# Routed rows withheld at the end of two outer stages, and a folded forward transform for two sequences

## The chip, the cores and the metric

The kernel runs on one core of one Trainium2 chip. The metric is the device time of one execution in microseconds. The kernel before took 2111.44 us, the median of three runs (2107.42 to 2115.52).

## What is computed

A long convolution over four sequences of 11456 positions and 128 channels (u = x v, convolved with a filter that a small MLP makes of position embeddings, the result multiplied by x), and a mixture of eight experts on the 45824 rows that come out, each row going to the one expert with the highest gate logit:

```python
h_filt = (np.maximum(pos_emb @ w1, 0.0) @ w2) * np.exp(-0.01 * pos)[:, None]
u = x * v
y = np.fft.irfft(np.fft.rfft(u, n=2 * S, axis=1) * np.fft.rfft(h_filt, n=2 * S, axis=0)[None], n=2 * S, axis=1)[:, :S]
x = (x * y).reshape(B * S, D)

logits = x @ w_gate + modality_bias[modality_id]
e_idx = np.argmax(logits, axis=1)
gate_w = softmax(logits)[np.arange(N), e_idx]
for e in range(E):
    h = np.maximum(x[e_idx == e] @ w1[e], 0.0)
    out[e_idx == e] = gate_w[e_idx == e, None] * (h @ w2[e])
```

## The kernel before, in words

The transform is cut into 90 x 64 and done as matmuls. The program is a row of stages. Filter stages make the filter; `filter_middle` (23 groups) writes its spectrum. Then for each sequence b an *outer* stage of 16 steps and a *middle* stage of 23 groups follow: outer 0 (the forward transform of sequence 0, laid under `filter_middle` with its loads and products), middle 0, outer 1, middle 1, outer 2, middle 2, outer 3, middle 3, outer 4, and last the expert tiles, in which 512 sorted rows at a time run through an expert's two matrices.

An outer stage b has two halves of work in each step. Of sequence b it does the forward transform (`forward_stages`): loads of u and v, `product` on DVE (L490), matmuls against the table `fwd` (L505, in `transform`, 64 instructions a step in two halves of 32), and the copy of each half out of PSUM by ACT (L508). Of sequence b - 1 it does the inverse transform (`inverse_stages`: turns L730, matmuls into `py` L739, ACT's copy L742, the sum and difference of the halves and the product with x on DVE, L743, L745, L746) and the routing (`route_stages`: L778 to L883; POOL's part are the gate's bias and the shift, L808 and L810; TensorE's transposes are L778 and L801).

The forward matmul takes its input with all 128 partitions; two of its 128 x 64 tiles lie side by side in the array.

A middle stage's group multiplies by the spectrum: matmuls L646, products on DVE (L663, L670) and POOL (L665, L666, L676, L677), inverse matmuls L701, copies L707.

Routing gives each row of a sequence its place in the sorted array `xs`. The rows go there by indirect DMAs that POOL issues, 90 for each sequence (`send_rows`, L283), each of 128 rows; they are loaded back first, five at a time (L263, here called `back`). How many rows go at which point is written by hand: `paced(x, n)` sends n rows that wait for instruction x. `product` sends two or three, the inverse transform two in each step, the last one also three in every second; some steps of the middle stages send more; and the loop over the expert tiles sends one in every second chunk for the first tiles, then one in every third:

```python
def paced(x, n=1):
    send_rows(n, wait=ins_of(x))
```

The order on TensorE, ACT, DVE and SP is the one in which the code is written, step by step: the tables `OUTER`, `LAST` and `FIRST` say at which step after its start each piece of work is done, and the place in the table says the order within a step. POOL's order is made by a scheduler.

In the expert loop each tile loads its rows (SP, L1121 for the tiles known early, L1125 and L1126 for the others), transposes them (L1210 on TensorE in the first tiles, L1212 on DVE later), and runs the matmuls. The results go out over DVE, SP's `y`, POOL's product with the gate weight (L1290) and four indirect DMAs (L1292, issued by POOL too). A load of x waits for the rows that may lie in it. After the last rows SP writes pads behind each expert's rows (L1052 and nine of L1060, in `rest`), and the x loads of later tiles stand behind these pads in SP's queue.

Of the kernel before, what the change touches and what calls it, by code (L numbers as in the profile page):

```python
# [48 lines left out]
def surely_full(n):  # L49
# [6 lines left out]
RW = D + 2  # L56
NOWHERE = 1 << 20
OUTER = ("turn0:2 turn1:2 lturn:5 biased:5 send:6 half:4 forward:3 load_x:0 product:2 choice:5 "
         "inverse:2 logits:4 shift:4 load:0 store:6 places:7")
LAST = ("lturn:5 biased:5 send:6 turn0:1 choice:5 turn1:1 inverse:2 logits:4 half:3 shift:4 load_x:0 store:5 places:6")  # L60
FOUT = "load:0 hidden:2 transform:3"
FMID = "turn:0 spectrum:1 second:3"
FIRST = "forward load product"
EA = 3
F1, F2 = 1, 24
UNSURE = 5
# [1 line left out]
NDYN = 8  # L68
NA, NXO = 12, 3
NPE = 9  # L70


def apart(a, axis):
# [116 lines left out]
def hyena_moe_kernel(ctx: ExitStack, tc: tile.TileContext, a: dict, out: bass.AP,  # L190
# [188 lines left out]
    with ExitStack() as cv:  # L379
# [93 lines left out]
        def forward_stages(b):  # L473
            kept = {}

            def load(q):
                for name in ("u", "v"):
                    if b == 0 and name == "v":
                        of = xo_t[q // 2 % NXO].rearrange("p w s h r -> p (w s h r)")
                        t = of[:, 1024 * (q % 2):1024 * (q % 2) + 1024]  # L480
                    else:
                        t = new_a((name, q))
                    kept[q, name] = t
                    sp.dma_start(t[0:D:2], a[name][b, q, 0:D // 2])
                    sp.dma_start(t[1:D:4], a[name][b, q, D // 2:])

            def product(q):

                u = kept[q, "u"]
                s = dve.scalar_tensor_tensor(u, u, sm("held")[:, 0:1], kept.pop((q, "v")),  # L490
                                             op0=ALU.mult, op1=ALU.mult)
                paced(s, 2 + (q % 2 == 0))
                if b:
                    free(("v", q))

            def transform(q):

                u = kept.pop((q, "u")).rearrange("p (b d n) -> p b d n", b=2, n=N2)
                for h in range(2):
                    p = pair("s1")  # L500
                    v = p[:, :, 0:4 * N1].rearrange("p b (d k) -> p b d k", d=4)
                    for j in range(4):
                        for blk in range(2):
                            for c in range(2):
                                pe.matmul(v[64 * c:64 * c + 64, blk, j], u[:, blk, 4 * h + j],  # L505
                                          fwd[:, c], start=True, stop=True)
                    d0 = 8 * q + 4 * h
                    act.copy(A.rearrange("p k b d -> p b k d")[:, :, :, d0:d0 + 4],  # L508
                             v.rearrange("p b d k -> p b k d"))
                free(("u", q))  # L510

            return load, product, transform

        def filter_stages():

# [201 lines left out]
        def inverse_stages(b):  # L717
# [15 lines left out]
            def transform(q):  # L733


                py = pair("py")
                for c in range(2):
                    for blk in range(2):
                        pe.matmul(py[64 * blk:64 * blk + 64, c], inv[:, c], w_of(q, blk)[:, c],  # L739
                                  start=True, stop=True)  # L740
                y = new_a(("y", q))
                act.copy(y[:, 512:1024], py[:, 1])  # L742
                paced(dve.tensor_add(y[:, 0:512], py[:, 0], y[:, 512:1024]),  # L743
                      1 + (b == nb - 1 and q % 2))
                dve.tensor_sub(y[:, 512:1024], py[:, 0], y[:, 512:1024])  # L745
                paced(dve.tensor_mul(xo_of(b, q // 2)[:, :, q % 2, :, 0:D], four(y),  # L746
                                     four(kept.pop(q))))
                free(("x", q), ("y", q))

            return load, turn, transform  # L750
# [147 lines left out]
        def outer_steps(b):  # L898
# [11 lines left out]
                    "choice": every_other(choice), "send": every_other(send),  # L910
                    "store": every_other(store), "places": every_other(places)}
            if b < nb:
                load, product, transform = forward_stages(b)
                todo |= {"load": load, "product": product, "forward": transform}
            if b == nb:
                todo.pop("places")
                for name, n in (("half", 2), ("logits", 2), ("lturn", 4), ("biased", 4), ("choice", 4),
# [9 lines left out]
                    lambda late: None, lambda late: (send(o), places(o))])  # L927
            if b == 0:
                ahead = lambda q: 2 * q if q < NA else q + F2 - NA
                when = {"load": ahead, "product": lambda q: ahead(q) + 2, "forward": lambda q: q + F2 - 1}  # L930
                return steps(NQ, [(when[n], todo[n]) for n in FIRST.split()])
            table = [w.split(":") for w in (LAST if b == nb else OUTER).split()]

# [157 lines left out]
    def experts(lo, hi):  # L1091
# [212 lines left out]
        for at in range(len(work) + 6):  # L1304
# [7 lines left out]
                finale[at - FL](late)  # L1312
            if lo == 0 and at >= FL + len(finale) + 2 and len(waiting) <= RC and not fetched:
                fetched.append(fetch(nb - 1))
            if lo == 0 and c % (2 if i < 12 else 3) == 0:
                send_rows(1)
            if lo == 0 and 1 <= i and c % 3 == 0:
                whole_weights(1)
# [31 lines left out]

def device_inputs(inputs):
    arrays = {name: np.ascontiguousarray(inputs[name]) for name in _INS}
    tile4 = lambda a: a.reshape(D, 2, NQ, 4, -1).transpose(2, 0, 1, 3, 4).reshape(NQ, D, -1)
    held = np.r_[0:D:2, 1:D:4]
    chan8 = lambda a: (apart(a.reshape(2, 64, 2, N2, NQ, 8), 1).transpose(4, 2, 1, 0, 5, 3)
                       .reshape(NQ, D, -1)[:, held])
    for name, of, order in (("x", "x", tile4), ("u", "x", chan8), ("v", "v", chan8)):
        arrays[name] = np.ascontiguousarray(
            np.stack([order(spread(np.asarray(a))) for a in inputs[of]]))

    pos = apart(spread(np.asarray(inputs["pos_emb"])).reshape(2, 64, 2, NQ, 4, -1), 1)
    arrays["pos_emb"] = np.ascontiguousarray(
# [24 lines left out]
```

## Time and profile before

| | before |
|---|---|
| median of three runs | 2111.44 us (2107.42 to 2115.52) |
| the profiled execution | 2110.57 us, span 2108.7 us, granted clock 0.986 of full speed |
| PE busy | 2022.3 us, 96% |
| weight loads (PEld) | 1653.7 us, 78% |
| DVE busy | 1675.1 us, 79% |
| ACT busy | 1192.9 us, 57% |
| POOL busy | 1369.1 us, 65% |
| HBM | 179 GB/s over the span |

The span runs from the first to the last instruction of the profiled execution; its own time is 1.9 us longer. Busy shares are averages over stages that differ: POOL's 65%, for instance, is made of stretches in which it has next to nothing to do and others in which it issues DMAs without a break.

### The profile page before, as it was taken

The numbers are of one execution on the slowest core, as the hardware profiler recorded it, in microseconds if no ns is written. First come the engines' busy times: TensorE is split into PE (matmuls) and PEld (weight loads), VectorE is DVE, ScalarE is ACT, GpSimd is POOL, SyncE is SP. The second block draws the span as 40 slices with busy tenths as digits, with TensorE's granted clock in tenths as the row PEclk, the third lists the DMA queues.
The fourth block names the chain that finished last, engine by engine and source line by source line (L and its number), as shares of the span: only waits on it lengthen the run. The fifth ranks groups of instructions, "written<-read, shape, count | busy, mean of one in ns | idle before, by whom it ended". The sixth has DMA issues, their size and how long they took to land. (4 is left out here: it accounts for less than half of the span.)

```text
span 2108.7 us, 49645 instructions
## 1 busy us (share of the span) xinstructions
PE 2022.3 (96%) x17794; PEld 1653.7 (78%) x17794; DVE 1675.1 (79%) x2663; ACT 1192.9 (57%) x2174; POOL 1369.1 (65%) x1496
## 2 busy tenths in 40 slices
PE   8999999999978999699999999999999999999997
PEld 8887877777757877488668888888888888888897
DVE  2538867996767967497887899988999999899885
ACT  3642476226631266223766666666666666666775
POOL 2219600796778876787667887888888665555554
PEclk9999999999989999899999999999999999999998
DMA  9846766678975788666689466666655554554310
GB/s 290 304 167 237 244 205 185 229 250 271 286 234 190 255 267 278 195 228 215 182 261 305 106 132 131 133 133 134 136 132 125 122 113 96 100 99 99 81 41 30
DMA packets 502932, 380.74 MB, mean 181 GB/s; under 512 B 374745, under 2 KB 408365, under 8 KB 502681
## 3 DMA queue, kind: packets, MB, share of 16 engines
q1 hardware_dynamic: 470265, 294.16, 51.0%
q0 software_dynamic: 32256, 83.33, 11.8%
q8 instruction: 142, 2.33, 0.4%
q14 instruction: 109, 0.89, 0.1%
q10 hardware_dynamic: 160, 0.03, 0.0%
HBM read 273.80 MB, written 103.96 MB: 179 GB/s over the span
## 5 line engine op out<-in xcount | busy, mean ns | idle before, releaser
L1240 DVE SCALAR_TENSOR_TENSOR hl<-ph,hh 128x512 fp32r<-128x512 f32 x724 | 484.7, 680 | 93.9 <-ACT hh L1239 85.0
L1239 ACT ACTIVATE hh<-ph 128x512 fp32r<-128x512 f32 x724 | 424.5, 598 | 200.9 <-PE ph L1236 193.1
L283 POOL DMA_INDIRECT xs<-back,to x360 | 389.4, 1082 | 175.8 <-issue 87.2
L1292 POOL DMA_INDIRECT out<-ot,idx x362 | 392.1, 1083 | 128.6 <-issue 82.0
L1234 PE MATMUL ph<-xh,wh 128*128 128x512 f32 (+1 forms) x792 | 298.5, 377 | 1.1 <-ACT xh L1220 1.1
L1236 PE MATMUL ph<-xl,wh 128*128 128x512 f32 (+1 forms) x792 | 296.1, 374 | 2.4 <-DVE xl L1221 2.4
L1235 PE MATMUL ph<-xh,wl 128*128 128x512 f32 (+1 forms) x792 | 294.4, 372 | 1.0 <-DVE wl L1189 1.0
L1257 PE MATMUL po<-hh,wh 128*128 128x512 f32 (+1 forms) x792 | 294.4, 372 | 0.0
L1259 PE MATMUL po<-hl,wh 128*128 128x512 f32 (+1 forms) x792 | 293.9, 371 | 0.0
L1258 PE MATMUL po<-hh,wl 128*128 128x512 f32 (+1 forms) x792 | 293.7, 371 | 0.0
L701 PE MATMUL pw<-rings,a 64*128 64x128 f32 x3952 | 242.1, 278 | 38.0 <-POOL a L676 33.9
L701 PEld LDWEIGHTS pw<-rings,a 64*128 64x128 f32 x3952 | 230.6, 191 | 57.3 <-POOL a L676 36.4
L707 ACT COPY A<-pw 128x512 f32<-128x512 f32 x180 | 95.7, 584 | 317.7 <-PE pw L701 317.7
L670 DVE TENSOR_TENSOR a<-pz,rings 128x1024 f32<-128x1024 f32 (+1 forms) x184 | 211.5, 1191 | 1.0 <-POOL a L677 1.0
L646 PE MATMUL pz<-A,rings 128*64 128x256 f32 x1440 | 170.0, 384 | 13.4 <-issue 8.9
L1236 PEld LDWEIGHTS ph<-xl,wh 128*128 128x128 f32 x792 | 149.4, 189 | 31.0 <-DVE xl L1221 3.5
L505 PE MATMUL s<-fwd,a 128*64 128x90 f32 x4096 | 170.1, 242 | 1.2 <-issue 1.1
L1235 PEld LDWEIGHTS ph<-xh,wl 128*128 128x128 f32 x792 | 149.6, 189 | 26.3 <-DVE wl L1189 1.3
L1234 PEld LDWEIGHTS ph<-xh,wh 128*128 128x128 f32 x792 | 149.4, 189 | 26.3 <-ACT xh L1220 1.3
L1257 PEld LDWEIGHTS po<-hh,wh 128*128 128x128 f32 x792 | 149.1, 188 | 26.0 <-issue 0.7
L1259 PEld LDWEIGHTS po<-hl,wh 128*128 128x128 f32 x792 | 149.1, 188 | 25.8
L1258 PEld LDWEIGHTS po<-hh,wl 128*128 128x128 f32 x792 | 149.1, 188 | 25.3
(192 smaller groups left out, 3537.7 us busy)
## 6 DMA issues: line engine op xcount, KB each, us to landing
rings<-hs SPq DMA_DIRECT2D x88, 512.0 KB
a<-in_x SPq DMA_DIRECT2D x64, 512.0 KB
xr<-xo SPq DMA_DIRECT2D x64, 365.6 KB
back<-xr POOLq DMA_DIRECT2D x72, 325.0 KB
rings<-in_c_b SPq DMA_DIRECT2D x88, 256.0 KB
rings<-in_c_c SPq DMA_DIRECT2D x88, 256.0 KB
x<-xs SPq DMA_DIRECT2D x292, 64.0 KB
ob<-oT SPq DMA_DIRECT2D x292, 64.0 KB
```

The costliest lines, as they stand in the source:

```text
L283: s = pool.indirect_dma_start(out=xs, out_offset=bass.IndirectOffsetOnAxis(ap=ix, axis=0), in_=src, in_offset=None, bounds_check=E * R - 1 ...
L670: dve.tensor_mul(part[i], z[:, :, i].unsqueeze(1).broadcast_to([D, 2, n, 2, D]), h[:, 0].unsqueeze(3).broadcast_to([D, 2, n, 2, D]))
L701: pe.matmul(pw[par][:, to:to + D], t[at], k["c"][at, q, c], start=i == 0, stop=i == len(terms) - 1)
L1234: pe.matmul(p, k[0, "h"][:, f:f + D], k["xh"], start=True, stop=False)
L1235: pe.matmul(p, k[0, "l"][:, f:f + D], k["xh"], start=False, stop=False)
L1236: pe.matmul(p, k[0, "h"][:, f:f + D], k["xl"], start=False, stop=True)
L1239: act.activation(hh, ph, AF.Relu)
L1240: dve.scalar_tensor_tensor(hl, ph, 0.0, hh.bitcast(F32), op0=ALU.max, op1=ALU.subtract)
L1257: pe.matmul(po, k[1, "h"][:, f], hh[:, t], start=g == 0, stop=False)
L1258: pe.matmul(po, k[1, "l"][:, f], hh[:, t], start=False, stop=False)
L1259: pe.matmul(po, k[1, "h"][:, f], hl[:, t], start=False, stop=g == NCH - 1)
L1292: s = pool.indirect_dma_start(out=out, out_offset=bass.IndirectOffsetOnAxis(ap=k["idx"][:, j:j + 1], axis=0), in_=ot[:, j, :], in_offset=N ...
```

## The change

Three things.

- `QS = 13`: steps 13 to 15 of outer 2 and outer 3 send no rows (neither from `product` nor from the inverse transform); those of outer 4 go on, at three in each step.
- The expert loop sends a row in every second chunk for the first 28 tiles, not 12.
- `FOLDED = 2`: for sequences 0 and 1 the host lays the two halves of a step's data beside each other, with one half's order turned. After `product`, POOL subtracts them (128 x 512), and DVE makes the sum of them (`total`, 128 x 512, as 2 times the one minus the difference). The forward matmuls take 64 partitions each, in four 64 x 64 tiles of the array instead of two of 128 x 64. There are as many of them as before.

```diff
 OUTER = ("turn0:2 turn1:2 lturn:5 biased:5 send:6 half:4 forward:3 load_x:0 product:2 choice:5 "
-         "inverse:2 logits:4 shift:4 load:0 store:6 places:7")
+         "inverse:2 total:2 logits:4 shift:4 load:0 store:6 places:7")
-FIRST = "forward load product"
+FIRST = "forward load product total"
+FOLDED = 2
+QS = 13
...
                 s = dve.scalar_tensor_tensor(u, u, sm("held")[:, 0:1], kept.pop((q, "v")),
                                              op0=ALU.mult, op1=ALU.mult)
-                paced(s, 2 + (q % 2 == 0))
+                paced(s, 2 + (q % 2 == 0) if q < QS else 0)
                 if b:
                     free(("v", q))
+                if b < FOLDED:
+                    pool.tensor_sub(u[:, 512:1024], u[:, 0:512], u[:, 512:1024])
+
+            def total(q):
+
+                u = kept[q, "u"]
+                if b < FOLDED:
+                    dve.scalar_tensor_tensor(u[:, 0:512], u[:, 0:512], 2.0, u[:, 512:1024],
+                                             op0=ALU.mult, op1=ALU.subtract)
...
                             for c in range(2):
-                                pe.matmul(v[64 * c:64 * c + 64, blk, j], u[:, blk, 4 * h + j],
-                                          fwd[:, c], start=True, stop=True)
+                                if b < FOLDED:
+                                    at = slice(64 * blk, 64 * blk + 64)
+                                    x, w = u[at, c, 4 * h + j], fwd[at, c]
+                                else:
+                                    x, w = u[:, blk, 4 * h + j], fwd[:, c]
+                                pe.matmul(v[64 * c:64 * c + 64, blk, j], x, w, start=True, stop=True)
...
-                paced(dve.tensor_add(y[:, 0:512], py[:, 0], y[:, 512:1024]),
-                      1 + (b == nb - 1 and q % 2))
+                n = 1 if b == nb - 1 or q < QS else 0
+                paced(dve.tensor_add(y[:, 0:512], py[:, 0], y[:, 512:1024]), n + (b == nb - 1))
                 dve.tensor_sub(y[:, 512:1024], py[:, 0], y[:, 512:1024])
                 paced(dve.tensor_mul(xo_of(b, q // 2)[:, :, q % 2, :, 0:D], four(y),
-                                     four(kept.pop(q))))
+                                     four(kept.pop(q))), n)
...
-                when = {"load": ahead, "product": lambda q: ahead(q) + 2, "forward": lambda q: q + F2 - 1}
+                when = {"load": ahead, "product": lambda q: ahead(q) + 2,
+                        "total": lambda q: ahead(q) + 3, "forward": lambda q: q + F2 - 1}
...
-            if lo == 0 and c % (2 if i < 12 else 3) == 0:
+            if lo == 0 and c % (2 if i < 28 else 3) == 0:
                 send_rows(1)
...
+    def chan8(a, b):
+        a = apart(a.reshape(2, 64, 2, N2, NQ, 8), 1)
+        if b < FOLDED:
+            a = np.stack([a[0], a[1][:, ::-1]]).transpose(4, 0, 1, 2, 5, 3)
+        else:
+            a = a.transpose(4, 2, 1, 0, 5, 3)
+        return a.reshape(NQ, D, -1)[:, held]
```

How the order moves, at three places. A row names the line, the operation, what it writes and reads, and how many alike stand together.

POOL, from the end of outer 2 to the first products of middle 2 (`xs<-back` is a routed row, `back<-xr` the load of five, L808 and L810 belong to the routing, `a` are the products' tiles). Before, rows stand up to the first product of group 0:

```order
L283 DMA xs<-back_95,to_92 373248x130 x2
L808 TENSOR_TENSOR lg<-wf,bias 109x128
L810 TENSOR_TENSOR lg<-lg,flagged 109x128
L283 DMA xs<-back_95,to_92 373248x130
L808 TENSOR_TENSOR flagged<-wf,bias 109x128
L283 DMA xs<-back_96,to_92 373248x130 x2
L263 DMA back_94<-xr_58 128x650
L283 DMA xs<-back_96,to_92 373248x130 x3
L283 DMA xs<-back_94,to_92 373248x130 x2
```

In the changed kernel:

```order
L285 DMA xs<-back_95,to_92 373248x130 x2
L265 DMA back_96<-xr_58 128x650
L285 DMA xs<-back_95,to_92 373248x130 x2
L823 TENSOR_TENSOR lg<-wf,bias 109x128
L825 TENSOR_TENSOR lg<-lg,flagged 109x128
L823 TENSOR_TENSOR flagged<-wf,bias 109x128
L823 TENSOR_TENSOR lg<-wf,bias 109x128
L825 TENSOR_TENSOR lg<-lg,flagged 109x128
L680 TENSOR_TENSOR a_125<-a_125 128x256
L681 TENSOR_TENSOR a_125<-a_125 128x256
L691 TENSOR_TENSOR a_128<-a_128,a_131 128x512
```

The rows have gone from between the routing's operations; five of these stand ahead of the first product (L665 before, L680 now).

DVE, one step of outer 1 (L490 is the product, `py` the inverse transform's result in PSUM, `xo` the step's output). Before:

```order
L743 TENSOR_TENSOR a10_133<-py_3611,a10_133 128x512
L745 TENSOR_TENSOR a10_133<-py_3611,a10_133 128x512
L746 TENSOR_TENSOR xo1_89<-a10_133,a6_129 128x2x4x128
L817 TENSOR_TENSOR lg_3626<-lt_3660,lg_3626 109x128
L490 SCALAR_TENSOR_TENSOR a0_123<-a0_123,small_81,a9_132 128x1024
```

In the changed kernel:

```order
L492 SCALAR_TENSOR_TENSOR a10_133<-a10_133,small_81,a0_123 128x1024
L759 TENSOR_TENSOR a5_128<-py_3445,a5_128 128x512
L760 TENSOR_TENSOR a5_128<-py_3445,a5_128 128x512
L761 TENSOR_TENSOR xo0_88<-a5_128,a9_132 128x2x4x128
L504 SCALAR_TENSOR_TENSOR a10_133<-a10_133 128x512
L832 TENSOR_TENSOR lg_3461<-lt_3495,lg_3461 109x128
L492 SCALAR_TENSOR_TENSOR a11_134<-a11_134,small_81,a2_125 128x1024
```

`total` (L504) works on the product of the same step (tile a10) and stands behind the three operations of the inverse.

POOL, expert tiles between the twelfth and the twenty-seventh. Before, three rows stand between two tiles (the last three operations of one tile are the cast of its indices L1280, the product L1290 and the four output DMAs L1292):

```order
L283 DMA xs_66<-back2_96,to1_93 373248x130 x3
L1280 CAST idx_20462<-ends_20233 128x4
L1290 TENSOR_TENSOR ot_20343<-y_20295,ends_19770 128x512
```

In the changed kernel four:

```order
L285 DMA xs_66<-back0_94,to0_92 373248x130 x2
L285 DMA xs_66<-back1_95,to0_92 373248x130 x2
L265 DMA back2_96<-xr2_60 128x650
L1296 CAST idx_15386<-ends_15147 128x4
L1306 TENSOR_TENSOR ot_15260<-y_15212,ends_14673 128x512
L1308 DMA out_0<-ot_15260,idx_14913 45824x128 x4
```

Eighteen rows more lie in this loop than before: 177 instead of 159 of the 360.

## Rows read from the trace of the kernel before

**Rows 1.** The page, busy tenths of PE in 40 equal slices of the span

```profile
PE   8999999999978999699999999999999999999997
```

**Rows 2.** Timeline of PE: start us, us, engine, line, operation, output<-inputs, count [idle before <-releaser]

```profile
369.40 0.47 PE L801 MATMUL lt<-ident,lT_late 128*109 128x128 f32 x2 [0.64 <-ACT lT_late L795]
...
483.61 0.34 PE L730 MATMUL wt<-ident,A 128*90 128x128 f32 x1 [0.61 <-DVE A L707]
...
604.63 0.36 PE L801 MATMUL lt<-ident,lT_late 128*109 128x128 f32 x1 [0.64 <-ACT lT_late L795]
...
637.41 0.58 PE L701 MATMUL pw<-rings,a 64*128 64x128 f32 x2 [16.58 <-POOL a L676]
...
736.54 0.34 PE L730 MATMUL wt<-ident,A 128*90 128x128 f32 x1 [0.64 <-DVE A L707]
...
857.60 0.36 PE L801 MATMUL lt<-ident,lT_late 128*109 128x128 f32 x1 [0.64 <-ACT lT_late L795]
...
988.71 0.34 PE L730 MATMUL wt<-ident,A 128*90 128x128 f32 x1 [0.64 <-DVE A L707]
```

**Rows 3.** Timeline of POOL and DVE at the start of middle 2

```profile
596.42 0.98 POOL L283 DMA_INDIRECT xs<-back,to  x1 [0.30 <-DVE score L833]
...
613.62 0.67 DVE L663 TENSOR_TENSOR a<-pz,rings 128x512 f32<-128x512 f32 x1
...
632.89 0.74 POOL L665 TENSOR_TENSOR a<-a 128x256 f32<-128x256 f32 x1
```

**Rows 4.** Timeline of POOL, SP and DVE in the expert tiles

```profile
1207.37 0.60 POOL L263 DMA_DIRECT2D back<-xr  x1
...
1212.65 1.03 POOL L1290 TENSOR_TENSOR ot<-y,ends 128x512 f32<-128x512 f32 x1
...
1636.91 0.97 POOL L283 DMA_INDIRECT xs<-back,to  x1 [0.30 <-issue]
...
1638.04 1.04 POOL L1290 TENSOR_TENSOR ot<-y,ends 128x512 f32<-128x512 f32 x1
...
1640.17 0.37 SPq L1052 DMA_DIRECT2D xs<-pad  x1
...
1663.47 0.71 DVE L1212 STREAM_TRANSPOSE xT<-x 128x512 f32<-128x512 f32 x1 [1.11 <-DMA x<-xs]
```

**Rows 5.** Timeline of SP, POOL and PE at the start of the expert tiles

```profile
1067.09 0.33 SPq L1121 DMA_DIRECT2D x<-xs  x1
...
1072.27 0.46 POOL L810 TENSOR_TENSOR bs_late<-bs_late,flagged 109x128 f32<-109x128 f32 x1
...
1072.65 0.66 PE L1210 MATMUL px<-ident,x 128*128 128x128 f32 x4
```

**Rows 6.** Groups by line, 95 to 160 us: count | busy, mean ns | idle before, releaser

```profile
L505 PE MATMUL s<-fwd,a 128*64 128x90 f32 x1024 | 40.4, 241 | 1.2 <-issue 1.1 <-DVE rings L609 0.2
L508 ACT COPY A<-s 128x720 f32<-128x720 f32 x32 | 24.3, 760 | 17.0 <-PE s L505 17.0
...
L676 POOL TENSOR_TENSOR a<-a,a 128x512 f32<-128x512 f32 x3 | 3.8, 1266 | 0.7 <-DVE a L670 0.7
```

**Rows 7.** Timeline of PE, ACT and DVE in outer 1

```profile
302.65 1.89 PE L739 MATMUL py<-rings,inv 90*64 90x512 f32 x8
...
304.59 0.59 ACT L742 COPY a<-py 128x512 f32<-128x512 f32 x1 [0.96 <-PE py L739]
305.21 0.70 DVE L743 TENSOR_TENSOR a<-py,a 128x512 f32<-128x512 f32 x1 [2.35 <-ACT a L742]
...
306.67 1.23 DVE L746 TENSOR_TENSOR xo<-a,a 128x1024 f32<-128x1024 f32 x1
...
308.46 2.70 PE L505 MATMUL s<-fwd,a 128*64 128x90 f32 x64
...
324.32 0.92 PE L505 MATMUL s<-fwd,a 128*64 128x90 f32 x18
```

**Rows 8.** Groups by line, first from 385 to 440 us, then from 295 to 330

```profile
L877 DVE TENSOR_TENSOR score<-score,oh 109x128 f32<-109x128 f32 x2 | 3.3, 1668 | 0.0
...
L877 DVE TENSOR_TENSOR score<-score,oh 109x128 f32<-109x128 f32 x2 | 0.6, 284 | 0.0
```

More of the change, by code (lines that the diff above doesn't have):

```diff
@@ L510, in transform @@
                 free(("u", q))
-            return load, product, transform
+            return load, product, total, transform
         def filter_stages():
@@ L912, in outer_steps @@
             if b < nb:
-                load, product, transform = forward_stages(b)
-                todo |= {"load": load, "product": product, "forward": transform}
+                load, product, total, transform = forward_stages(b)
+                todo |= {"load": load, "product": product, "total": total, "forward": transform}
             if b == nb:
@@ L1352, in device_inputs @@
     arrays = {name: np.ascontiguousarray(inputs[name]) for name in _INS}
-    tile4 = lambda a: a.reshape(D, 2, NQ, 4, -1).transpose(2, 0, 1, 3, 4).reshape(NQ, D, -1)
+    tile4 = lambda a, b: a.reshape(D, 2, NQ, 4, -1).transpose(2, 0, 1, 3, 4).reshape(NQ, D, -1)
     held = np.r_[0:D:2, 1:D:4]
-    chan8 = lambda a: (apart(a.reshape(2, 64, 2, N2, NQ, 8), 1).transpose(4, 2, 1, 0, 5, 3)
-                       .reshape(NQ, D, -1)[:, held])
+    def chan8(a, b):
[5 more added lines that the diff above has]
+        return a.reshape(NQ, D, -1)[:, held]
     for name, of, order in (("x", "x", tile4), ("u", "x", chan8), ("v", "v", chan8)):
         arrays[name] = np.ascontiguousarray(
-            np.stack([order(spread(np.asarray(a))) for a in inputs[of]]))
+            np.stack([order(spread(np.asarray(a)), b) for b, a in enumerate(inputs[of])]))
     pos = apart(spread(np.asarray(inputs["pos_emb"])).reshape(2, 64, 2, NQ, 4, -1), 1)
```

## Prediction

> **What bounds the kernel now.** I read first the line of busy tenths over the span: PE is full, nine tenths or more, from the eighteenth of the forty slices on, which holds the end of middle 3, the last outer stage and all expert tiles but the end, and dips in slices 12, 13 and 17 [rows 1]. So TensorE bounds the kernel, and time can come back only where it stands still: in those dips, and in stretches where a faster matmul shortens PE's own work.
>
> Then the timeline of PE at both ends of each middle stage [rows 2]. From the last step of an outer stage (L801) to the first of the next (L730) it takes 483.61 - 369.40 = 114.2 us in middle 1, 736.54 - 604.63 = 131.9 in middle 2 and 988.71 - 857.60 = 131.1 in middle 3. The same groups are done in all three; the last two cost 17.7 and 16.9 more, and the row at 637.41 shows where: the inverse matmul (L701) stood 16.58 us for POOL's product L676.
>
> Then POOL at the same place [rows 3]. It sends routed rows (L283) one after the other from 596.42 on, and comes to the first product of middle 2 (L665) only at 632.89, though DVE did its half of that work (L663) at 613.62: POOL is some 18 us behind with rows.
>
> Last, the expert tiles round the end of the rows [rows 4]. The program on POOL is full there: from the `mul` of tile 9 (1212.65) to that of tile 47 (1638.04) a tile takes 425.39 / 38 = 11.19 us. The last row goes at 1636.91 and lands about 3 us later, just when SP writes the pads (L1052 at 1640.17), and the x loads behind the pads end so late that DVE's transpose of x waited 1.11 us for one (1663.47). That wait is the whole reserve of the tile, used up.
>
> **No rows in the last three steps.** Thirteen rows leave each of outer 2 and 3, so POOL has nothing but L808 and L810 between the last row of step 12 and L665. Before, rows and shifts from 596.42 to 632.89 took 36.5 us; the product then waits for DVE alone, as in middle 1. Both surpluses go: **gain 17.7 + 16.9 = 35 us** (bounds 30 to 36; the low one if some rows still lie between). Nothing else in these outer stages is gained, since there PE and not POOL is awaited.
>
> The 26 rows aren't saved. Outer 4 sends three in each step and gets back eight, so 18 rows more are left for the expert tiles: 177 instead of 159.
>
> **Their price in the expert tiles.** A row costs 0.97 + 0.30 = 1.27 us of POOL, a load of rows (`back`, L263, one for five rows) 0.60 [rows 4]. Between `mul` 9 and 47 lie 115 rows and 23 loads, so a tile's own work (`mul`, four scatters of the output, the cast) is (425.39 - 115 x 1.27 - 23 x 0.60) / 38 = 7.0 us. In the change tiles 9 to 26 send four rows instead of three, the last row comes after `mul` 47 instead of before it: 133 rows, 26.6 loads and 39 tiles, 133 x 1.27 + 26.6 x 0.6 + 39 x 7.0 = 458 us. The last row goes 458 - 425 = 32 us later against the tiles. There is no cover: the pads on SP wait for the last rows, the x loads stand behind the pads, and PE waits for x. I add 1 to 2 us for matmuls at the lower clock after such a stall: **loss 33.5**. Bounds: 15 if x loads issued ahead still feed PE for a tile and a half, 38 if waits of the loads of rows add a sixth. I take the value by the rows, since POOL was already the later engine.
>
> **The start of the expert tiles.** SP issues the first x load at 1067.09, some 2 us of reserve before PE's first transpose at 1072.65 [rows 5]. This load must follow all rows known to it, now up to row 180. In the change that row is sent in the last step but two of outer 4, behind the shifts on POOL (the last at 1072.27), so the load leaves at 1073 to 1075, lands some 3 later, and PE starts near 1081: **loss 8.5** (bounds 4 and 12, by whether two or five rows lie behind those shifts). SP queues its other x and weight loads behind the waiting one.
>
> **Four tiles in outer 0.** The forward matmuls of one half are 32 of 1024, 40.4 x 32 / 1024 = 1.26 us; ACT's copy takes 0.76 and waits for PE [rows 6]. With 64 by 64 tiles the array holds four at once instead of two. No row shows this shape, so I bound it: no gain at all, or half, 0.62. With half, the two PSUM buffers and ACT set the pace: two halves cost 0.62 + 0.27 + 0.76 + 0.07 = 1.7 us, 0.87 each (0.27 and 0.07 are the handoffs that I estimate from the copies' waits), 32 x (1.26 - 0.87) = 12. The new work on the way is a subtraction on POOL (as L676, 1.27) and DVE's `total` (half of L490's kind, about 0.66) in sixteen steps under filter_middle, where both have room but for a few; I take 2 off. **Gain 10** (bounds -2 and 13). The Trainium skill (TensorE: Matmul & The Clock Gate, "Wait — 56ns, not 53.3ns?") gives 25 ns as the least start-to-start; by it a half would be 0.80 us and the gain 8, and no run here shows it.
>
> **Folding in outer 1.** There PE is in a row without gaps: the forward starts at 308.46 and again at 324.32, 15.86 us for two steps [rows 7]. Two halves at 0.63 saved each could give 16 steps x 1.26 = 20 at most, were PE all. But a loop closes: `total` now stands on DVE behind the inverse's three operations and ahead of the next product. L505 of the next step waits for it, the copies of L508 free the PSUM that `py` (L739) needs, ACT's L742 follows `py` (start 302.65 to copy's end 305.18: 2.5), and the DVE operations up to xo's end take 306.67 + 1.23 - 305.21 = 2.7. With 1.72 from forward's start to the freed buffer and 0.66 for `total` a step is 1.72 + 2.5 + 2.7 + 0.66 = 7.6, a little under PE's 7.9. The subtraction on POOL comes on top: L877, two SBUF operands on DVE, took a mean of 284 ns in outer 1 and of 1668 in the stretch round the start of middle 1, where POOL works on products [rows 8]. I charge 1.0 in every second step, that is 16.3 against 15.9 in each of some six full pairs of steps, and 2 for the stage's short first steps: **loss 5** (bounds: gain 2, if nothing collides, loss 9). The Trainium skill (SBUF — State Buffer, "Who interferes with whom") says that a DVE instruction with two SBUF inputs and a GpSimd one that reads SBUF shut each other out for the whole instruction. By that rule, which rows 8 bear out, every step could grow by the 1.27 of the subtraction to 8.9, a us over PE's 7.9, and the loss would be 15; without it there would be none.
>
> **Sum.** Profiled run 2110.6: -35 -10 +5 +8.5 +33.5 = +2, **2113 us**; that run lies 0.9 under the median, which I leave. A half per cent, 10.6 us, is about what can be told from no change, so the forecast is "same"; its own range is 2100 to 2126.
>
> **Rivals.** *A, the backlog never reaches PE.* If the x loads don't hang on the last rows (enough are issued ahead, or POOL's scatters run at less than 1.27 when the tile's own work is spread), the 33.5 go away: 2079. For it: PE is full through all tiles though POOL fell behind since tile 9. Against it: the pads left at 1640.17, just as the last row landed, and x was then waited for. *B, the four tiles are no faster than two.* Then outer 0 loses 2 instead of gaining 10 (12 apart), and in outer 1 the freed PSUM comes 0.6 later in each of 16 steps, 10 more: 2113 + 12 + 10 = 2135, slower. It decides as soon as a half takes over 1.2 us. For it: no row of this shape; against: the two-tile rows pack without gaps. *C, the rows stay in the way:* POOL's scheduler puts other work, or leftover rows, ahead of L665, and the middle starts cost what they did, 2148. Against it speaks the changed order, in which only five small operations stand there.
>
> **Chances.** Forecast 0.54 (0.08 of it faster by over 0.5%, 0.40 within, 0.06 slower), A 0.28, B 0.12, C 0.06. Faster 0.08 + 0.28 = 0.36, same 0.40, slower 0.06 + 0.12 + 0.06 = 0.24. The range of 8 in 10 takes in A with some play and the forecast's own bounds, and leaves out most of B and C: 2070 to 2132.
>
> **What would show it.** Right: middle 2 and 3 at 114 us from L801 to L730; L505 in outer 0 under 30 us busy; a two-step period of 16 to 16.5 in outer 1; the first x load at 1073 or later against the end of outer 4; the last row some 32 us later against `mul` 9, and a stall of PE of some 30 us at an x of tile 50 to 54. Wrong: no such stall (A), L505 with starts as far apart as before (B), or L701 waiting 16 us for L676 (C).

## The result: slower by 1.3%, and the profile after

Median 2139.16 us (2136.42 to 2143.32, four runs) against 2112.68 us of the kernel before, run beside it: 1.013 times as long, 95% interval 1.0105 to 1.0155. That is 26.5 us slower; the profiled execution has a span of 2141.5 us, 32.8 over the one before. The profiled execution is the slowest of the four. The forecast was 2113 us and "same", in a range of 2070 to 2132.

The page's slices show where PE still dips, and where newly. First the busy tenths of PE and its granted clock in the changed kernel:

```profile
PE   8989988999989998999799999999999599999997
...
PEclk9999998999999999999999999999999799999998
```

The dips of slices 12, 13 and 17 [rows 1] have shrunk: slices 12 and 16 stand at 8 tenths. New are slice 3 (outer 0), slices 6 and 7 (outer 1, the second of them with a lower clock), slice 20 (the end of outer 4) and slice 32 (inside the expert tiles).

The places at which the prediction cut the program, in the timeline of PE: the first turn (L745, L730 before) of outer 1, 2, 3 and 4 and the first transpose of the tiles (L1226, L1210 before). The changed kernel:

```profile
245.08 0.34 PE L745 MATMUL wt<-ident,A 128*90 128x128 f32 x1 [0.64 <-DVE A L722]
...
492.63 0.34 PE L745 MATMUL wt<-ident,A 128*90 128x128 f32 x1 [0.61 <-DVE A L722]
...
732.98 0.34 PE L745 MATMUL wt<-ident,A 128*90 128x128 f32 x1 [0.61 <-DVE A L722]
...
974.90 0.34 PE L745 MATMUL wt<-ident,A 128*90 128x128 f32 x1 [0.64 <-DVE A L722]
...
1073.69 0.47 PE L1226 MATMUL px<-ident,x 128*128 128x128 f32 x1 [12.24 <-DMA x<-xs]
```

and of the kernel before the one that isn't among [rows 2, 5]:

```profile
248.63 0.34 PE L730 MATMUL wt<-ident,A 128*90 128x128 f32 x1 [0.64 <-DVE A L707]
```

The differences of neighbouring rows are the lengths of the stretches (us; the last reaches to the end of the span):

| stretch | before | after | change | forecast |
|---|---|---|---|---|
| up to outer 1 | 248.6 | 245.1 | -3.6 | -10 |
| outer 1, middle 1 | 235.0 | 247.6 | +12.6 | +5 |
| outer 2, middle 2 | 252.9 | 240.3 | -12.6 | -17.7 |
| outer 3, middle 3 | 252.2 | 241.9 | -10.2 | -16.9 |
| outer 4, up to the first x | 83.9 | 98.8 | +14.9 | +8.5 |
| expert tiles | 1036.1 | 1067.8 | +31.8 | +33.5 |

Every sign is the forecast one, and the largest term comes out near its size. The other four terms of the sum (outer 2 and 3 are one term) came out worse than forecast by 6 to 12 us each, and these make the 31 us between +2 and +32.8.

**The tiles.** Timeline of POOL, SP, DVE and PE in the changed kernel, the counterpart of [rows 4]:

```profile
1213.58 1.07 POOL L1306 TENSOR_TENSOR ot<-y,ends 128x512 f32<-128x512 f32 x1
...
1670.63 0.98 POOL L285 DMA_INDIRECT xs<-back,to  x1 [0.30 <-issue]
...
1672.97 0.37 SPq L1068 DMA_DIRECT2D xs<-pad  x1
...
1680.02 0.72 DVE L1281 STREAM_TRANSPOSE oT<-po 128x512 f32<-128x512 f32 x1 [13.12 <-DMA ob<-oT]
...
1681.37 0.80 PE L1275 MATMUL po<-hl,wh 128*128 128x512 f32 x1 [12.23 <-DVE off L333]
...
1690.96 0.35 SPq L1141 DMA_DIRECT2D x<-xs  x1
...
1694.81 0.71 DVE L1228 STREAM_TRANSPOSE xT<-x 128x512 f32<-128x512 f32 x1 [12.84 <-DMA x<-xs]
...
1696.14 0.80 PE L1275 MATMUL po<-hl,wh 128*128 128x512 f32 x1 [11.85 <-DVE off L335]
```

The last row goes 1670.63 - 1213.58 = 457.0 us after `mul` 9; before it was 424.3, so 32.8 later, against 32 worked out. The first pad follows its landing (1672.97). PE then stands still twice, 12.23 and 11.85 us, and only the second time for an x load. The first time DVE's transpose of a result (L1281) waits 13.12 us for the store of an earlier result (`ob<-oT`), which SP issues at 1676.31, behind the first pads; PE waits for what stands behind that transpose on DVE. The second time the x load stands behind the pads (1690.96), DVE's transpose of x waits 12.84 us for it, and PE again for what stands behind. (The releaser that the PE rows name, L333 and L335, is only the operation ahead on DVE's queue; the DVE rows tell the cause.) Over the whole of the tiles PE is idle 25.3 us longer than before and busy 6.4 us longer (1022.96 for 1016.50), with the clock at its lower level behind the waits: 0.5 granted from 1680 to 1700.

**The ends of outer 2 and 3.** The first product of middle 2 (L680, L665 before) no longer stands behind rows; POOL waits for DVE:

```profile
629.71 0.72 POOL L680 TENSOR_TENSOR a<-a 128x256 f32<-128x256 f32 x1 [2.20 <-DVE a L678]
```

The stretch that the prediction named, from the last step of the outer stage (L816, L801 before) to the next first turn, starts here:

```profile
618.19 0.36 PE L816 MATMUL lt<-ident,lT_late 128*109 128x128 f32 x1 [0.64 <-ACT lT_late L810]
...
864.54 0.36 PE L816 MATMUL lt<-ident,lT_late 128*109 128x128 f32 x1 [0.64 <-ACT lT_late L810]
```

With the first turns above that is 732.98 - 618.19 = 114.8 us in middle 2 and 974.90 - 864.54 = 110.4 in middle 3, against 131.9 and 131.1 before. But the outer stages ahead of it, from their first turn to L816, have grown: outer 2 takes 125.6 us (121.0 before) and outer 3 131.6 (121.1). In them a wait has grown. POOL, DVE and PE near the end of outer 3:

```profile
844.48 0.98 POOL L285 DMA_INDIRECT xs<-back,to  x1 [6.24 <-DMA back<-xr]
...
849.61 0.98 POOL L285 DMA_INDIRECT xs<-back,to  x1 [0.30 <-issue]
...
851.11 0.45 POOL L825 TENSOR_TENSOR lg<-lg,flagged 109x128 f32<-109x128 f32 x1
...
851.59 0.29 DVE L832 TENSOR_TENSOR lg<-lt,lg 109x128 f32<-109x128 f32 x1 [11.80 <-POOL lg L825]
...
851.94 0.47 PE L745 MATMUL wt<-ident,A 128*90 128x128 f32 x1 [5.35 <-DVE lg L832]
```

The last rows before step 13 are still being sent; behind them on POOL stands the routing's shift (L825). The routing's next operation on DVE (L832) waits 11.80 us for it, and DVE does its queue in order, so the inverse transform of the next step stands too, and PE 5.35 us, with the clock at its lower level after it (0.50 granted from 852 to 860). At the end of outer 2 L832 waits 6.35 us in the same way. About half of the 11.80 us isn't the sending itself: POOL stood 6.24 us for the load of five rows that it had issued at 836.34.

**Outer 1.** Timeline of PE, POOL and DVE in six steps:

```profile
284.91 0.31 PE L521 MATMUL s<-fwd,a 64*64 64x90 f32 x4 [1.86 <-DVE a L504]
...
303.64 0.31 PE L521 MATMUL s<-fwd,a 64*64 64x90 f32 x4 [1.30 <-DVE a L504]
...
312.78 1.27 POOL L498 TENSOR_TENSOR a<-a 128x512 f32<-128x512 f32 x1 [5.62 <-DVE a L492]
...
313.01 1.19 DVE L844 TENSOR_TENSOR lg<-lg,mx 109x128 f32<-109x128 f32 x1
...
319.84 0.31 PE L521 MATMUL s<-fwd,a 64*64 64x90 f32 x4 [1.87 <-DVE a L504]
...
321.57 3.68 PE L754 MATMUL py<-rings,inv 90*64 90x512 f32 x8
...
338.19 0.31 PE L521 MATMUL s<-fwd,a 64*64 64x90 f32 x4 [1.30 <-DVE a L504]
```

PE waits for `total` (L504) nine times in the stage, from 284.91 on ahead of the forward of every second step, 14.8 us in all. The two steps from 303.64 to 319.84 take 16.2 us, as forecast (16.3), but the pair before them takes 18.7 and the pair behind them 18.4; before, pairs in the steady part of the stage took 15.6 to 15.9. While POOL subtracts (L498, 1.27), the one DVE operation with two operands that starts under it, L844, takes 1.19 us; in outer 2, where POOL subtracts nothing, it takes 0.29. What the forecast lacked is in the row at 321.57: the eight matmuls into `py` take 3.68 us where they took 1.89 [rows 7], the lower of PE's two clock levels (1.2 GHz for 2.4). The windows 245 to 360 us, before and after (length, busy us and instructions of PE, PEld, DVE, ACT, POOL, granted clock, DMA share, GB/s):

```profile
245.00:360.00 115.00, 114.36 (x1501) 86.53 (x1498) 77.20 (x137) 78.44 (x144) 7.37 (x17) 1.00 0.66 211
```

```profile
245.00:360.00 115.00, 98.97 (x1347) 64.73 (x1347) 82.27 (x136) 71.02 (x130) 24.16 (x29) 0.93 0.63 196
```

**Outer 0.** The forward matmuls, groups by line from 95 to 165 us, and two stretches of them:

```profile
L521 PE MATMUL s<-fwd,a 64*64 64x90 f32 x1024 | 28.0, 260 | 9.0 <-issue 3.4 <-ACT A L523 3.3 <-ACT rings L622 1.3
```

```profile
105.65 4.36 PE L521 MATMUL s<-fwd,a 64*64 64x90 f32 x128 [0.79 <-DVE rings L624]
110.26 1.51 PE L521 MATMUL s<-fwd,a 64*64 64x90 f32 x64 [0.25 <-ACT A L523]
```

They are faster, 28.0 us busy for 40.4 [rows 6], so rival B's ground is not there. But PE now has gaps, 9.0 us, and part of the stage ran at the lower level: 128 in 4.36 us are 34 ns each, 64 in 1.51 are 24.

### The profile page after: what moved, and what is told of

Same layout as the page of the kernel before. It is cut to its first block, busy times and chain, and to the rows that moved or that the text cites. A ratio compares the mean times of both kernels' runs of the same rounds, so it can differ in the third digit from the quotient of the medians.

```text
span 2141.5 us, 49730 instructions
## 1 busy us (share of the span) xinstructions
PE 2013.5 (94%) x17794; PEld 1625.6 (76%) x17794; DVE 1700.2 (79%) x2695; ACT 1189.9 (56%) x2174; POOL 1413.6 (66%) x1528
## 5 line engine op out<-in xcount | busy, mean ns | idle before, releaser
L285 POOL DMA_INDIRECT xs<-back,to x360 | 393.9, 1094 | 172.2 <-issue 87.3
L716 PE MATMUL pw<-rings,a 64*128 64x128 f32 x3952 | 237.5, 275 | 4.9 <-ACT A L722 1.4
L1252 PEld LDWEIGHTS ph<-xl,wh 128*128 128x128 f32 x792 | 149.5, 189 | 31.8 <-DVE xl L1237 4.3
L521 PE MATMUL s<-fwd,a 64*64 64x90 f32 (+1 forms) x4096 | 143.1, 252 | 25.2 <-DVE a L504 14.8
```

Source lines behind the costliest of these rows:

```text
L285: s = pool.indirect_dma_start(out=xs, out_offset=bass.IndirectOffsetOnAxis(ap=ix, axis=0), in_=src, in_offset=None, bounds_check=E * R - 1 ...
L716: pe.matmul(pw[par][:, to:to + D], t[at], k["c"][at, q, c], start=i == 0, stop=i == len(terms) - 1)
L1252: pe.matmul(p, k[0, "h"][:, f:f + D], k["xl"], start=False, stop=True)
```

## The experiments

All are edits of the changed kernel. "Before" is the kernel before, run beside each.

**e1, folding alone.** `QS = 16`, and the rows of outer 4 and of the tiles as before:

```diff
-QS = 13
+QS = 16
...
-                paced(dve.tensor_add(y[:, 0:512], py[:, 0], y[:, 512:1024]), n + (b == nb - 1))
+                paced(dve.tensor_add(y[:, 0:512], py[:, 0], y[:, 512:1024]), n + (b == nb - 1 and q % 2))
...
-            if lo == 0 and c % (2 if i < 28 else 3) == 0:
+            if lo == 0 and c % (2 if i < 12 else 3) == 0:
```

> Only the folded transform for two sequences; rows sent as in the kernel before. Theory (terms add, as read from the two traces): outer 0 gains some 6 us, outer 1 loses some 12, about 2119 us (2114 to 2124), with the first x load and the pads as before. Rival (outer 1 lost because of rows on POOL or of the changed order there, not because of the folding): outer 1 no longer than before, about 2107.

Measured 2115.52 against 2111.88 us, ratio 1.0024 (1.0012 to 1.0036): inside what the theory gave.

**e2, rows alone.** `FOLDED = 0`.

> Only the rows: none in the last three steps of outer 2 and 3, one in every second chunk for 28 expert tiles; no folding. Theory: the starts of middle 2 and 3 give 23 us, the late first x load takes 15, the pads 29: about 2134 us (2128 to 2140), with PE waiting about 12 us for the first x and some 25 to 30 us round tile 53. Rival (the row part is even, the folding is the whole loss): 2108 to 2118.

Measured 2131.88 us, 1.0091 (1.0072 to 1.0109), inside what the theory gave. The two parts together give 1.0115; the change has 1.013. They add, and four fifths of the loss are the rows. e1's outer 1 and middle 1 take 486.83 - 242.26 = 244.6 us, 9.6 more than before, with the rows as they were: the loss there is the folding's. First turns of e1, then of e2 (outer 2, 3, 4) and e2's first x:

```profile
242.26 0.34 PE L745 MATMUL wt<-ident,A 128*90 128x128 f32 x1 [0.65 <-DVE A L722]
...
486.83 0.34 PE L745 MATMUL wt<-ident,A 128*90 128x128 f32 x1 [0.61 <-DVE A L722]
```

```profile
481.92 0.34 PE L745 MATMUL wt<-ident,A 128*90 128x128 f32 x1 [0.61 <-DVE A L722]
...
720.77 0.34 PE L745 MATMUL wt<-ident,A 128*90 128x128 f32 x1 [0.64 <-DVE A L722]
...
963.04 0.34 PE L745 MATMUL wt<-ident,A 128*90 128x128 f32 x1 [0.64 <-DVE A L722]
...
1062.52 0.45 PE L1226 MATMUL px<-ident,x 128*128 128x128 f32 x1 [12.52 <-DMA x<-xs]
```

**e3, the rows alone with later pads.** e2 and:

```diff
-            if NW1 - 10 <= i < NW1:
+            if NW1 - 6 <= i < NW1:
                 next(others, 0)
```

> The rows alone, and the pads (with the table behind them) begun four tiles later. Theory (PE's stall in the tiles is x loads queued behind pads that wait for the last rows, nothing else): the stall of some 29 us goes, about 2105 us (2100 to 2110), and POOL's last row comes as late as without it. Rival (POOL's backlog itself holds PE, through the results' tiles or SP's queue): the stall stays, 2125 to 2136.

Measured 2116.93 us, 1.002 (1.0008 to 1.0032): between the two. The trace is of an execution of 2110.52 us, near the fastest of the nine. In it the last row goes at 1650.34 and the first pad at 1676.07, so the pads don't wait for rows any more, and the tiles take 2108.7 - 1052.85 = 1055.9 us, 15 less than in e2 (2133.1 - 1062.52 = 1070.6) but 20 more than before. Of these 20 us PE is idle for 9.5 and busy longer for 10.3. The pads' own row on SP, some 24 us from the first to the last, is as long as in the kernel before; PE waits 3.15 us there. What the rest hangs on, no run shows. The last row, the first pad and that wait:

```profile
1650.34 1.50 POOL L285 DMA_INDIRECT xs<-back,to  x1 [0.30 <-issue]
...
1676.07 0.37 SPq L1068 DMA_DIRECT2D xs<-pad  x1
...
1701.03 0.80 PE L1275 MATMUL po<-hl,wh 128*128 128x512 f32 x1 [3.15 <-DVE off L335]
```

**e4, folding alone, the sum ahead of the inverse.** e1 and:

```diff
 OUTER = ("turn0:2 turn1:2 lturn:5 biased:5 send:6 half:4 forward:3 load_x:0 product:2 choice:5 "
-         "inverse:2 total:2 logits:4 shift:4 load:0 store:6 places:7")
+         "total:2 inverse:2 logits:4 shift:4 load:0 store:6 places:7")
```

> The folded transform alone, with the sum of the halves on DVE ahead of the inverse's operations instead of behind them. Theory (outer 1 is held by the loop forward, copy, inverse, sum, forward): the loop is cut, outer 1 takes at most what it took before, and up to 15 us less: 2095 to 2108 us. Rival (it is held by DVE operations shut out while POOL subtracts, or by the lower clock of the smaller tiles): outer 1 stays some 12 us longer than before, 2116 to 2124.

Measured 2100.33 us, 0.9953 (0.9936 to 0.997). Outer 1 and middle 1 take 470.88 - 242.56 = 228.3 us, 16 less than in e1 and 7 less than before. DVE now waits for POOL's subtraction, in time that it spent waiting for `py` anyway, and the clock stays at its upper level in 245 to 360:

```profile
311.18 0.69 DVE L504 SCALAR_TENSOR_TENSOR a<-a 128x512 f32<-128x512 f32 x1 [1.47 <-POOL a L498]
```

```profile
245.00:360.00 115.00, 107.66 (x1606) 72.78 (x1608) 97.09 (x163) 81.53 (x151) 27.18 (x33) 1.00 0.69 211
```

The subtraction and the small tiles are the same in e1 and e4, and so is the shut-out (L844 takes 1.20 in e4 too); only the place of `total` differs. So the place of `total` was the cause, and the lower clock came with it. What the 0.9 us of the shut-out added in the old place, no run tells.

**f1 to f4 and g1 to g4.** These ran on two chips on which the kernel before itself took 2166.7 and 2155.1 us, so only ratios count. f1 withholds rows in outer 2 alone, without folding:

```diff
-                paced(s, 2 + (q % 2 == 0) if q < QS else 0)
+                paced(s, 2 + (q % 2 == 0) if q < QS or b != 2 else 0)
...
-                n = 1 if b == nb - 1 or q < QS else 0
+                n = 1 if b != 1 or q < QS else 0
...
-            if lo == 0 and c % (2 if i < 28 else 3) == 0:
+            if lo == 0 and c % (2 if i < 17 else 3) == 0:
```

> No folding; the rows are withheld in outer 2 only, outer 3 sends as before, and 17 instead of 28 expert tiles send in every second chunk (five rows more than before are left for the tiles). Theory: the start of middle 2 keeps its 14 us, middle 3 loses its gain, the first x load waits 0 to 2 us since 13 rows more are out, the pads cost 5 rows and a tile, some 7: about 2105 us (2099 to 2110). Rival (any row taken out of an outer stage comes back in full later): 2112 to 2118, with a wait for the first x.

Ratio 1.0033 (0.9996 to 1.0069): can't be told from no change, and not the gain of the theory. The kernels of f2, f3 and f4 (their edits are at h1, h3 and h2 below, which ran them on a chip with 2110.7 us for the kernel before) came back as g2, g3 and g4:

> The same rows, and the folding with the sum of the halves ahead of the inverse. Theory (the terms add): 2100.3 - 14 + 7 = 2093 us (2088 to 2098). Rival (POOL's subtractions or the earlier stages shift the rows and undo one of the two): 2098 to 2108.

> The kernel of f2 again, on another chip. As for f2: the terms add, 2093 us (2088 to 2098); rival 2098 to 2108.

f2 gave 0.9987 (0.9958 to 1.0016), which can't be told from no change, and g2 0.9963 (0.9931 to 0.9995), a small gain. As ratios to 2111.9 us the theory's range is 0.989 to 0.993 and the rival's 0.993 to 0.998, so on these two chips the theory missed.

> No folding; no rows from step 11 on in outer 2 and 3, four in each step of outer 4, 46 expert tiles with a row in every second chunk, pads four tiles later. Read by the stretch from the first turn of outer 2 to the first of outer 3: 252.9 us before, 238.9 with rows withheld from step 13 on. Theory (what is left of the stall is DVE waiting for the routing's shift, which POOL does behind rows that are late): with nine rows fewer the stall in the last step goes, 232 to 236. Rival (it is the lower clock, or a late load of rows): 237 to 241. The total (the first x load later still) about 2120 to 2145, not read.

> The kernel of f3 again, on another chip, read by the stretch from the first turn of outer 2 to the first of outer 3 as there. Theory (DVE waits for the shift behind late rows): 232 to 236 us; rival: 237 to 241.

One run each, 2210.42 and 2198.69 us. The kernel before takes longer on these chips too, so the stretch can't be read against 252.9 us. It can be read against f4 and g4 below, which withhold rows from step 13 on: 242.2 against 249.1 us on the one chip and 245.1 against 252.9 on the other, 6.9 and 7.8 less, as the theory wanted.

> The rows alone, with three and four rows in turn in outer 4's steps instead of three, and 21 expert tiles with a row in every second chunk. Theory (the first x load is late because row 180 is sent late, and the pads because eight rows more lie in the tiles): PE's wait for the first x falls from 12.5 to under 4 us, the last row comes 10 us earlier against the tiles, about 2113 us (2107 to 2120). Rival (POOL is full in outer 4, more rows in its steps only queue up and hold the shift that DVE waits for): row 180 no earlier, 2122 to 2134.

> The kernel of f4 again, on another chip. Theory: PE's wait for the first x falls from 12.5 to under 4 us, about 2113 us (2107 to 2120). Rival: row 180 no earlier, 2122 to 2134.

f4 2188.64 us in one run, g4 1.0039 (1.0013 to 1.0065). PE's wait for the first x was 0.3 us in both, yet outer 4 up to the first x took 99.6 and 99.5 us, as long as in e2 with its wait (99.5): the wait had moved, and the runs didn't tell the two views apart.

g1 put everything together: e4's order, e3's pads, and `(b == nb - 1) * (1 + q % 2)` rows more in outer 4.

> All pieces that the runs so far favour: folding for two sequences with the sum ahead of the inverse, no rows from step 13 on in outer 2 and 3, three and four rows in turn in outer 4's steps, 22 tiles with a row in every second chunk, pads four tiles later. Theory (terms add): folding -11.5 as in e4, middle starts -24 to -29, what is left of the first x load and of the tiles +15 to +20: about 2090 us (2082 to 2097). Rival (more rows in outer 4 only queue up on POOL): first x as late as in e3 and shift waits on top, 2100 to 2112.

Ratio 0.9998 (0.9963 to 1.0032): withholding rows in outer 3 as well, with more of them in outer 4, gave nothing over g2, and the theory's range, 0.986 to 0.993 of the kernel before, is missed.

**h1, f1's rows and e4's order.**

> The kernel of f2 and g2 a third time, wanted on a chip where the kernel before takes its 2112 us. Theory (the terms add): 18 us under e4's saving less 7, that is 16 to 24 us under the kernel before; rival: no better than e4, 8 to 13 under it.

Measured 2088.63 against 2110.72 us, 0.9895 (0.9871 to 0.992), 22 us under the kernel before, as the theory wanted. The gain depends on the chip: the same kernel as g2 gave 0.9963. Its rows show the balance: the first turns of outer 2, 3 and 4, a stall in middle 3, the first x.

```profile
474.68 0.34 PE L745 MATMUL wt<-ident,A 128*90 128x128 f32 x1 [0.64 <-DVE A L722]
...
715.52 0.34 PE L745 MATMUL wt<-ident,A 128*90 128x128 f32 x1 [0.64 <-DVE A L722]
...
868.55 0.59 PE L716 MATMUL pw<-rings,a 64*128 64x128 f32 x2 [13.42 <-POOL a L691]
...
967.10 0.34 PE L745 MATMUL wt<-ident,A 128*90 128x128 f32 x1 [0.64 <-DVE A L722]
...
1050.90 0.33 PE L1226 MATMUL px<-ident,x 128*128 128x128 f32 x1
```

Outer 2 and middle 2 take 240.8 (12 under before), outer 3 and middle 3 251.6 (as before, with the stall), outer 4 83.8 (as before: the first x no longer waits), the tiles 2087.2 - 1050.90 = 1036.3 (as before).

**h2, three and four rows in turn in outer 4,** rows alone:

```diff
-                paced(dve.tensor_add(y[:, 0:512], py[:, 0], y[:, 512:1024]), n + (b == nb - 1))
+                paced(dve.tensor_add(y[:, 0:512], py[:, 0], y[:, 512:1024]), n + (b == nb - 1) * (1 + q % 2))
...
-            if lo == 0 and c % (2 if i < 28 else 3) == 0:
+            if lo == 0 and c % (2 if i < 21 else 3) == 0:
```

> The kernel of f4 and g4 a third time. On the two chips before, PE's wait for the first x was 0.3 us, but outer 4 took longer there, so POOL had more time. Theory (row 180 is late for want of rows in outer 4's steps): the wait stays under 4 us where outer 4 is as short as in e2, and the kernel lies 0 to 8 us over the one before. Rival (POOL is full there): 8 us or more of wait, 14 or more over the one before.

Measured 2117.04 us, 1.0022 (1.0006 to 1.0038). The first x isn't waited for any more, yet outer 4 takes 1059.64 - 963.2 = 96.4 us where e2 takes 99.5 and the kernel before 83.9. The wait has moved to the one that the ends of outer 2 and 3 showed:

```profile
1050.22 0.29 DVE L832 TENSOR_TENSOR lg<-lt,lg 109x128 f32<-109x128 f32 x1 [7.56 <-POOL lg L825]
...
1052.38 0.29 PE L883 MATMUL pr<-oh,both 109*128 109x128 bf16 x1 [6.31 <-DVE oh L859]
```

Both views had half: row 180 was late, and POOL has little room in outer 4 for more. In the 17 us ahead of this shift POOL stood 3.70 and 2.11 us round loads of rows, so here too the loads have a part in it. The rest of the gain over e2 lies in the tiles, 12 us for eight rows fewer.

**h3, no rows from step 11 on** (rows alone; `QS = 11`, four rows in each step of outer 4, 46 tiles at every second chunk, e3's pads).

> The kernel of f3 and g3 a third time. Theory (what is left of the loss at the start of middle 2 and 3 is DVE's wait for the shift that POOL does behind late rows): no wait of DVE's L832 over 4 us in the last three steps, first turn of outer 2 to first turn of outer 3 in 232 to 236 us against 238.9 with rows withheld from step 13. Rival (lower clock, late loads of rows): 237 to 241.

```profile
486.29 0.34 PE L745 MATMUL wt<-ident,A 128*90 128x128 f32 x1 [0.61 <-DVE A L722]
...
718.72 0.34 PE L745 MATMUL wt<-ident,A 128*90 128x128 f32 x1 [0.65 <-DVE A L722]
...
834.51 0.29 DVE L832 TENSOR_TENSOR lg<-lt,lg 109x128 f32<-109x128 f32 x1 [9.00 <-POOL lg L825]
```

Outer 2 and middle 2 take 232.4 us, 6.4 less than in e2 and inside what the theory gave; the longest wait of L832 there was 4.4 us, a little over the 4 expected. In outer 3 it still waits 9.00 and the stretch is 238.3. So late rows ahead of the shift are the cause of what is left in outer 2. In outer 3 POOL sends the last row ahead of the shift at 827.95 and then stands 4.01 us at the next load of rows (L265, 832.94), whose wait the profile puts down to a row (DMA `xs<-back`); the shift stands behind that load. There the rival's late load has a part, and how much of the stall is rows and how much loads stays open. The total, 2160.76 us in one run, carries 21.8 us of waiting for the first x, and wasn't to be read.

**h4, h1 with e3's pads.**

> The kernel of h1 with the pads four tiles later. Theory (five rows more in the tiles still cost some 7 us at the pads): 5 to 8 us under h1. Rival (on the rows of h1 the pads no longer hold anything): same as h1 within 3 us.

Measured 2087.32 us, 0.9887 (0.987 to 0.9903), the best of all, and not told apart from h1: on h1's rows the pads hold nothing.

## Why the prediction was wrong, step by step

- **"Both surpluses go: gain 35."** The backlog at the product went, as said: middle 2 and 3 take 114.8 and 110.4 us where 114 was named, and rival C is out. The step that failed is "Nothing else in these outer stages is gained, since there PE and not POOL is awaited". It put at nothing what late rows do inside the outer stages: the shift stands behind them on POOL, DVE waits for the shift and PE for DVE, and outer 2 and 3 grew by 4.5 and 10.5 us. Gain 22.8; h3 gets 6.4 more in outer 2 by taking nine further rows out.
- **"Loss 5" in outer 1.** The kind was right (a loop through `total`, and the shut-out in every second step), the term too small: the loss was 12.6, or 9.6 in e1. The forecast took 16.3 us for every pair of steps; the pair at 303.64 took 16.2, its neighbours 18.7 and 18.4. It put the lower clock at nothing: behind some of the waits for `total` the clock fell (0.93 granted in the stretch). By the Trainium skill's rule (SBUF — State Buffer, "Who interferes with whom") the prediction gave a loss of 15, with every step grown by the subtraction's 1.27 us; the row shows one operation, L844, held 0.9 us in every second step. In the changed kernel these 0.9 us stand ahead of `total` in DVE's queue; e4 shows that they cost PE nothing where `total` stands ahead of the inverse.
- **"Loss 8.5" for the first x.** Right in kind, PE waited 12.24 us for that load, but mis-sized: the loss was 14.9. The prediction placed the load at 1073 to 1075 by the times of the kernel before, which is 84 to 86 us after the first turn of outer 4; it left 95.9 us after it (1070.78 - 974.90). POOL did the last shift (L825 at 1064.85) 90.0 us after that turn and not 83.6, having stood 4.49 us at a load of rows (L265 at 1051.91), and four rows lay behind the shift. (The forecast's own sum doesn't close either: 1075 and 3 for the landing are 1078, not 1081.)
- **"Gain 10" in outer 0.** Mis-sized. The matmuls took 28.0 us as against 20 by half and 40.4 by nothing, so the four tiles work, but only 5.2 us reached the end of the forward and 3.6 the start of outer 1. Part was lost to the clock, 0.96 granted from 80 to 120 us and 0.91 from 120 to 160, where it was 1.00 before. One pair of profiles is a weak measure here: outer 1 starts at 246.9 to 249.8 us in the ten traces without folding and at 242.3 to 245.1 in the eight with it, about 5 us apart in the mean.
- **"Loss 33.5" in the tiles.** The sum came out, 31.8, and the last row came 32.8 us later, as worked out; what it was made of didn't. The prediction let the whole 32 us reach PE ("There is no cover") through x loads behind the pads and added 1 to 2 for the lower clock. PE was idle 25.3 us longer and busy 6.4 longer, and half of the standing still came through the store of results behind the pads. So some 7 us of cover were there, and that the total is near is partly luck. Rival A falls: the backlog reached PE. That it comes through the pads, e3 and h1 show: with later pads the tiles lose 20 us (e3) in place of 35 (e2), and with fewer rows none (1036.3 us in h1, 1036.1 before).

Rival B's 2135 lies near the measured time, but not by its mechanism. The forecast's sum was a small difference between a gain of 45 and losses of 47; four of the five terms were off to the same side. The gain in the middle stages was taken at the length of the wait that it removes, and the waits added in outer 1 and ahead of the first x were priced without what stands behind them.

## What to carry to other kernels

When work is taken out of one stretch of a queue, look for everything that stands behind what remains there, on every engine that waits for it, and not only for the wait that was to go. A new operation between an engine's result and the next input belongs ahead of work that waits for something else anyway: the same folding lost 3.6 us behind the inverse and gained 11.5 ahead of it. Work that is deferred must have room where it goes; rows moved from outer 2 alone cost nothing later in h1, those of outer 3 came back in outer 4 and the tiles.

## What the runs showed of the hardware

The clock fell after quite short gaps, though not after each: in outer 1 PE stood 1.86 and 1.87 us ahead of the forwards at 284.91 and 319.84, and the `py` matmuls right behind them ran at half speed, 3.64 and 3.68 us for 1.89; behind the gaps of 1.30 us at 303.64 and 338.19, and behind one of 2.12 us at 253.42, they took 1.94. The granted clock over 245 to 360 us was 0.93; in e4, without these waits, it was 1.00. The length of a single gap doesn't tell which it is.

Matmuls in four 64 x 64 tiles in turn ran 64 in 1.47 us where the clock was up, that is 19 to 23 ns from start to start (by whether the last one's own time is counted). The Trainium skill (TensorE: Matmul & The Clock Gate, "Wait — 56ns, not 53.3ns?") gives about 25 ns as the least from start to start; across four tiles this run shows less. The row, from the changed kernel's outer 1:

```profile
295.72 1.47 PE L521 MATMUL s<-fwd,a 64*64 64x90 f32 x64
```
